# Attention of the later batches, one run a step or two runs every second step

## The chip, the cores and the metric

The kernel runs on one core of a Trainium2 chip. The metric is the device time of one execution in microseconds; the runs of a kernel are summarised by their median. A core has five engines that run beside each other, each through its own list of instructions in order: TensorE (PE in the profile, its weight loads PEld), VectorE (DVE), ScalarE (ACT), GpSimd (POOL) and SyncE (SP), which here issues the DMAs.

## The reference

Attention over 4 batches, 8 heads, 576 tokens and 64 dimensions, with a window of 32 keys: the first four heads see the last 32 keys ("plain"), the other four every fourth key of the last 128 ("dilated"). Two feed-forward blocks follow, over all 2304 tokens.

```python
scores = scale * np.matmul(q, k.transpose(0, 1, 3, 2))
scores = np.where(masks[None, :, :, :], scores, -1000000000.0)
attn = softmax(scores)                      # over the keys
x = np.matmul(attn, v)                      # then (tokens, 512)
x = ((x @ w_in) * np.cos(x @ w_in)) @ w_out # 512 -> 2048 -> 512
h = np.maximum(np.maximum(x @ w1, x @ w2), x @ w3)
return h @ w_out2                           # 512 -> 768 -> 512
```

## The kernel before

Attention is cut into 48 **runs** `(b, p, i)`: batch `b`, pair of heads `p` (0 and 1 plain, 2 and 3 dilated) and 192 queries `i`. A run has two query blocks of 96 and two heads, so four small problems of 96 queries by 128 keys. It goes through these operations, each a function of its own:

- `att_scores` (S): eight matmul instructions on TensorE at line 268 (four products in two passes each). The two heads lie in the two row halves of the array, and head `h` writes bank `6 + h` of PSUM. Then four reductions on VectorE (line 275) add the mask, take the row minimum of the negated scores and write the tile `e` in SBUF.
- `att_exp`: four exponentials on ScalarE (line 292, recorded at line 217). ScalarE loads a table when it goes from `Exp` to `Sin` or back, since the feed-forward block uses `Sin`.
- `att_norm`: an add, a reciprocal and one multiplication over `e` (lines 303 to 307).
- `att_T` (T): four transposes on TensorE (line 315) into one bank, and one copy to the tile `pt` (recorded at line 143).
- `att_out` (O): eight matmul instructions (line 326) into a bank, and then, for each piece of the destination, a copy and a subtraction into `ring` (lines 143 and 345). A dilated run has two or three pieces, a plain run mostly one. `att_done` calls it and then issues the load of the run five places on.

In the loop before, T of a run stands in bank 6 and O in bank 7; S uses both.

The first 12 runs are done ahead of the main loop. The main loop has 80 steps `s`, 16 for each of five token blocks (512 tokens, the last 256). A step has up to eight **chunks**: four "h" chunks of the first feed-forward product (three matmuls each, line 358) and four "a" chunks of the second (line 407) for the step three earlier. After the last h chunk `ff1_reduce` brings the argument into range on VectorE and ScalarE and issues the sine; `ff1_g` of the step before multiplies, and splits the product for the next matmul. In the second and third block `ff1_reduce` is done by VectorE in even steps and mostly by ScalarE in odd ones. In step `s` of the second to fourth block a piece of 256 columns of the last block's weights is also converted (lines 183, 443, 446).

The other 36 runs (12, 10, 12 and 2 of them during the first four blocks) are laid among the chunks. A run enters at the step that `LAST` spreads it to, which is nearly one run a step; its scores, transposes and outputs come at three places of a step, after the first, third and sixth chunk (T of the run three or two steps earlier, S of the new run, O of the earlier one). `GROUP` says how many runs share one `att_exp`: two in the first block, one in the others. The exponentials follow at the end of the step, the normalisation at the end of a later step.

The order in the code is a priority and not the order on the engines: the framework places instructions on an engine by that priority as they come ready, so that what waits is passed by what does not. It also adds the waits between engines, among them those on a PSUM bank that another engine reads.

Of the kernel before, what the change touches and what calls it, by code (L numbers as in the profile page):

```python
# [24 lines left out]
QB = 96  # L25
NQ = S // QB
KB = QB + WIN
# [3 lines left out]
NF1 = FF1 // 128  # L31
# [5 lines left out]
NBT = len(BLOCKS)  # L37
# [8 lines left out]
START = (3, 6, 7)  # L46
# [19 lines left out]
}  # L66


LAST = (13, 10, 12, 8)
GROUP = (2, 1, 1, 1, 1)  # L70

START_WEIGHTS = (0, 0, 2, 1, 0, 0, 0, 1, 0, 0, 1, 0, 1, 0, 1)
STEP_WEIGHTS = (
# [24 lines left out]
def body(  # L98
# [11 lines left out]
    nc = tc.nc  # L110
# [40 lines left out]
    bank = [ps.tile([128, 512], F32, name=f"bank{n}") for n in range(8)]  # L151
# [69 lines left out]
    given = {}  # L221
# [31 lines left out]
    places = {}  # L253
    HEADS = [(j, h) for j in range(2) for h in range(2)]

    def att_scores(u, n=None):
        b, p, i = u
        places[u] = (6, 7) if n is None else (START[2 * n % len(START)], START[(2 * n + 1) % len(START)])
        e = sp.tile([QB, 4, KB], F32, tag="e", name="e")

        m = smp.tile([QB, 4], F32, tag="m", name="m")
        places_of = {}
        for j, h in HEADS:
            q, k, _ = given[u][j]
            if n is None:
                rows = slice(64 * h, 64 * h + 64)
                sv = bank[6 + h][:QB, j * KB : j * KB + KB]
                nc.tensor.matmul(sv, q[rows], k[rows], start=True, stop=True)  # L268
            else:
                sv = bank[n % 3][:QB, (2 * j + h) * KB : (2 * j + h + 1) * KB]  # L270
                nc.tensor.matmul(sv, q[:, h * QB : (h + 1) * QB], k, start=True, stop=True)
            places_of[j, h] = sv
        for j, h in HEADS:
            kind = (PLAIN_KIND if p < 2 else DIL_KIND)[2 * i + j]
            nc.vector.tensor_tensor_reduce(  # L275
                out=e[:, 2 * j + h, :],
                in0=places_of[j, h],
                in1=mask[:, kind, :],
                scale=-1.0 / math.sqrt(D),
                scalar=3e38,  # L280
                op0=ALU.add,
                op1=ALU.min,
                accum_out=m[:, 2 * j + h : 2 * j + h + 1],
            )
        st[u] = e, m
# [547 lines left out]
    enter = {}  # L833
    for t, us in enumerate(plan[1:]):
        for i, u in enumerate(us):
            enter.setdefault(t * NF1 + i * LAST[t] // len(us), []).append(u)
    to_exp, to_norm, to_out = [], [], []
    NS = NBT * NF1
    hvs = {}
    for s in range(NS + LAG):  # L840
        phase[0] = 1 if s < NF1 else 2 if s < NS - NF1 else 3
        us = enter.get(s, [])
        assert s % NF1 or finished >= set(sum(plan[: s // NF1 + 1], []))
        if s == 0:
            weight_loads(WSLOTS, WSLOTS)

        vs = [to_out.pop(0) for _ in range(min(len(to_out), 1))]
        pieces = []
        for j in range(max(len(us), len(vs))):
            if j < len(vs):  # L850
                pieces.append((att_T, vs[j]))
            if j < len(us):
                pieces.append((att_scores, us[j]))
            if j < len(vs):
                pieces.append((att_done, vs[j]))
        chunks = []
        t, f = divmod(s, NF1)
        if s < NS:

            hv = (bank[3] if s == 2 else h_bank[(s + (s > 2)) % 2])[:, : BLOCKS[t]]  # L860
            hc = h_chunks(hv, halves[("in", f)], STARTS[t] % RING, BLOCKS[t])
            chunks += [("h", n, c) for n, c in enumerate((2, 3, 0, 1))]
        if s >= LAG:
            chunks += [("a", dm, 0) for dm in range(NC)]
        done = 0
        for j, (kind, x, c) in enumerate(chunks):
            if kind == "h":
                hc(x, c)
                if x == NC - 1:
                    hvs[s] = hv  # L870
                    ff1_reduce(s, hv)
            else:
                t0, f0 = divmod(s - LAG, NF1)
                acc_chunk(STARTS[t0], f0 == 0, f0 == NF1 - 1, halves[("out", f0)], g[s - LAG], x)
            while done < len(pieces) and done * len(chunks) < (j + 1) * len(pieces):
                do, u = pieces[done]
                do(u)
                done += 1
            if j == 1:
                if s >= 1 and s - 1 < NS:  # L880
                    ff1_g(s - 1)
            if s < NF1:
                weights(STEP_WEIGHTS[s].count(j), WSLOTS)
            if j == 1:
                raw_exponent(s - NF1)
            if j == 5:
                raw_bits(s - NF1)
        for u in us:
            to_exp.append(u)
        if to_norm:  # L890
            att_norm(to_norm, zt, tensor("norm"))
            to_out += to_norm
        to_norm = []
        if len(to_exp) >= GROUP[min(t, NBT - 1)] or (to_exp and s % NF1 >= LAST[min(t, len(LAST) - 1)]):
            zt = att_exp(to_exp)
            to_norm, to_exp = to_exp, []
        k = s - (NS - NF1)
        if k >= 0:
            ff2_early(k)
# [82 lines left out]
```

## Time and profile before

| | |
|---|---|
| time, median of 3 runs | 823.3 us (822.85 to 824.14) |
| profiled execution, span | 820.7 us |
| what lies around the span, median less span | 2.6 us |
| TensorE busy | 792.5 us, 97% |
| VectorE busy | 546.9 us, 67% |
| ScalarE busy | 463.7 us, 57% |
| GpSimd busy | 135.1 us, 16% |
| mean granted clock of TensorE | 0.983 of full speed |

The profile is of one execution, for which the span from its first to its last instruction is given; its own time is that span and what lies around it, which is taken from the runs. Busy times are unions of the engine's instructions. Matmuls are pipelined: a record lasts longer than the distance to the next one, so the price of a piece of TensorE's work is read from starts, not from durations.

### The profile page before, as it was taken

The page shows a single profiled execution, that of the slowest core. Times are in us where ns is not written, and L with a number is a line of the kernel's source. Part 1 is how long each engine was busy: PE and PEld are TensorE (multiplying, and loading weights), DVE is VectorE, ACT ScalarE, POOL GpSimd, SP SyncE. Part 2 cuts the span into 40 slices and gives each one's busy share as a digit, 9 for nine tenths or more (in the row PEclk, how much of TensorE's full clock was granted, in tenths as well). Part 3 has the DMA queues.
Part 4 walks back from the last instruction along what each step waited for, and adds up shares of the span by engine and source line. Part 5 has one row for each costly group of instructions (what it writes and reads, how often), then busy time and mean ns, then how long its engine had stood idle before and what let it go on. Part 6 is the DMA issues. An engine that isn't in the chain of part 4 may idle for free.

```text
span 820.7 us, 12988 instructions
## 1 busy us (share of the span) xinstructions
PE 792.5 (97%) x4484; PEld 679.5 (83%) x4484; DVE 546.9 (67%) x1442; ACT 463.7 (57%) x1063; POOL 135.1 (16%) x118
## 2 busy tenths in 40 slices
PE   8778999999999999999999999999999999999998
PEld 6556777777778777777788889998899999999997
DVE  5997698768886788876665477886872356515540
ACT  5787998868884488884553244364552233423321
POOL 2454345410000000000000002135510000000000
PEclk8987999999999999999999999999999999999999
DMA  9973111234344443332010025637683788448802
GB/s 350 419 283 142 39 48 52 73 113 148 117 129 130 128 163 112 115 121 84 27 45 10 0 94 183 238 144 271 239 311 106 225 248 263 150 135 254 253 26 77
DMA packets 52625, 124.43 MB, mean 152 GB/s; under 512 B 5840, under 2 KB 18768, under 8 KB 52560
## 3 DMA queue, kind: packets, MB, share of 16 engines
q1 hardware_dynamic: 52560, 123.61, 44.4%
q8 instruction: 35, 0.57, 0.3%
q14 instruction: 30, 0.25, 0.1%
HBM read 91.34 MB, written 32.24 MB: 151 GB/s over the span
## 4 chain that ended last, share of the span: by engine, by line
PE 77%; DVE 9%; DMA 8%; ACT 2%; issue 2%; POOL 1%; SPq 0%; DVEq 0%; ACTq 0%; POOLq 0%
PE bank L407 21%; PE bank L358 21%; PE bank L592 19%; PE bank L657 9%; DMA w<-in_w_in 4%; PE bank L268 4%; PE bank L326 2%; DMA raw<-wd 2%; PE bank L315 2%; DMA qkv<-in_qkv 2%; DVE ws L516 1%; DVE w L188 1%; POOL wa L491 1%; DVE e L307 1%; DVE wx L191 1%
## 5 line engine op out<-in xcount | busy, mean ns | idle before, releaser
L358 PE MATMUL bank<-ring,w 128*128 128x512 f32 (+1 forms) x960 | 236.1, 382 | 6.3 <-DVE r L396 5.1
L407 PE MATMUL bank<-gt,w 128*128 128x512 f32 (+1 forms) x960 | 223.7, 376 | 0.0
L592 PE MATMUL bank<-ring,wa 128*128 128x384 f32 x1134 | 201.3, 337 | 3.5 <-DVE mx L622 3.3
L592 PEld LDWEIGHTS bank<-ring,wa 128*128 128x128 f32 x1134 | 198.0, 189 | 5.1 <-DVE mx L622 4.1
L358 PEld LDWEIGHTS bank<-ring,w 128*128 128x128 f32 x960 | 165.2, 191 | 40.8 <-DVE r L396 6.6
L407 PEld LDWEIGHTS bank<-gt,w 128*128 128x128 f32 x960 | 165.8, 190 | 33.4 <-issue 0.6
L217 ACT ACTIVATE r<-r,hpi 128x512 f32<-128x512 f32 (+1 forms) x80 | 54.5, 681 | 70.0 <-DVE r L387 59.0
L217 ACT ACT_TABLE_LOAD x62 | 79.5, 1283 | 8.3 <-issue 3.4
L217 ACT ACTIVATE e<-e,m 96x128 f32<-96x128 f32 x192 | 74.8, 391 | 6.4 <-DVE m L275 6.0
L657 PE MATMUL bank<-g,w 128*128 128x384 f32 x432 | 76.3, 334 | 0.0
L657 PEld LDWEIGHTS bank<-g,w 128*128 128x128 f32 x432 | 75.0, 188 | 0.0
L396 DVE TENSOR_TENSOR r<-bank,r 128x512 f32<-128x512 f32 (+1 forms) x80 | 50.6, 632 | 27.2 <-ACT r L217 27.1
L139 POOL TENSOR_SCALAR gt<-r 128x512 fp32r<-128x512 f32 x24 | 16.3, 680 | 290.7 <-PE bank L407 132.5
L275 DVE CUSTOM_DVE_ANT_0 e<-bank,cs 96x128 f32<-96x128 f32 x192 | 44.9, 282 | 20.5 <-PE bank L268 9.2
L208 POOL TENSOR_TENSOR w<-wx,w 128x512 fp32r<-128x512 f32 x32 | 46.0, 1442 | 37.3 <-ACT w L143 34.0
L608 ACT COPY s<-bank 128x384 f32<-128x384 f32 x54 | 25.8, 478 | 39.0 <-PE bank L592 37.5
L398 DVE TENSOR_TENSOR gt<-r,gt 128x512 fp32r<-128x512 f32 (+1 forms) x65 | 40.3, 621 | 11.2 <-POOL gt L139 8.5
L626 DVE TENSOR_TENSOR s<-s,bank 128x384 f32<-128x384 f32 x36 | 19.8, 550 | 34.2 <-PE bank L592 34.2
L268 PEld LDWEIGHTS bank<-qkv 64*96 64x96 f32 x288 | 24.0, 168 | 20.2 <-issue 5.9
L626 DVE TENSOR_TENSOR mx<-s,bank 128x384 f32<-128x384 f32 x18 | 9.9, 550 | 43.2 <-PE bank L592 43.2
L382 DVE CUSTOM_DVE_ANT_0 r<-bank,r 128x512 f32<-128x512 f32 x40 | 27.4, 685 | 15.9 <-ACT r L381 15.7
L268 PE MATMUL bank<-qkv 64*96 64x128 f32 x288 | 35.4, 302 | 2.4 <-DVE m L275 2.4
(68 smaller groups left out, 908.7 us busy)
## 6 DMA issues: line engine op xcount, KB each, us to landing
wa<-opd SPq DMA_DIRECT2D x54, 512.0 KB, 4.5
opd<-wa SPq DMA_DIRECT2D x27, 512.0 KB, 3.0
qkv<-in_qkv SPq DMA_DIRECT2D x36, 336.0 KB, 2.9
wh<-in_w SPq DMA_DIRECT2D x36, 256.0 KB, 2.9
w<-in_w_in SPq DMA_DIRECT2D x16, 512.0 KB, 9.2
w<-in_w_out SPq DMA_DIRECT2D x16, 512.0 KB, 9.8
qkv<-in_qkv SPq DMA_DIRECT2D x12, 432.0 KB, 9.1
wd<-wh SPq DMA_DIRECT2D x36, 128.0 KB, 1.9
```

Of the source, the lines that this page charges most:

```text
L208: tensor("w_lo").tensor_tensor(out=w[:, 1, :], in0=x, in1=w[:, 0, :].bitcast(F32), op=ALU.subtract)
L217: last_table.append(nc.scalar.activation(*args, **kw).ins)
L268: nc.tensor.matmul(sv, q[rows], k[rows], start=True, stop=True)
L275: nc.vector.tensor_tensor_reduce(out=e[:, 2 * j + h, :], in0=places_of[j, h], in1=mask[:, kind, :], scale=-1.0 / math.sqrt(D), scalar=3e38 ...
L358: nc.tensor.matmul(hv, w[:, a, 128 * c : 128 * c + 128], ring[c][:, x, c0 : c0 + n_tok], start=n == 0 and j == 0, stop=n == NC - 1 and j == 2,
L382: nc.vector._custom_dve(dve_ops.TENSOR_ADD_SAT, out=r, in0=hv, in1=r, s0=ARG_HI, s1=ARG_LO)
L396: nc.vector.tensor_tensor(out=r, in0=hv, in1=r, op=ALU.mult)
L398: tensor("g_lo").tensor_tensor(out=gt[:, 1, :], in0=r, in1=gt[:, 0, :].bitcast(F32), op=ALU.subtract)
L407: nc.tensor.matmul(a_dm, w[:, a, 128 * dm : 128 * dm + 128], gt[:, x, :], start=first and n == 0, stop=last and n == 2,)
L592: nc.tensor.matmul(out, ops[q][a][:, x, 128 * c : 128 * c + 128], b_op(b, c)[:, y], start=first and c == 0 and n == 0, stop=c == 1 and n == 2,
L626: nc.vector.tensor_tensor(out=o, in0=y, in1=x, op=ALU.add)
L657: nc.tensor.matmul(a, wo[2 * f + r][:, x, 128 * dm : 128 * dm + 128], g2[f, r, n][:, y], start=f == 0 and r == 0 and k == 0, stop=f == NF2 ...
```

## The change

Runs enter in pairs at every second step. In such a step the transposes of both older runs stand together after the first chunk, the outputs of both after the fourth, and the scores of both new runs after the seventh. Run `k` of a pair now has bank `6 + k` for its transposes and its outputs; scores of head `h` stand in bank `6 + h` as before, the second run's 256 columns further. Exponentials of the pair follow at the end of the step, the normalisation at the end of the next, transposes and outputs in the one after that. `LAST` and `GROUP` go.

```diff
-LAST = (13, 10, 12, 8)
-GROUP = (2, 1, 1, 1, 1)
+PIECES = (0, 3, 6)
...
-    def att_scores(u, n=None):
+    def att_scores(u, n=None, k=0):
         b, p, i = u
-        places[u] = (6, 7) if n is None else (START[2 * n % len(START)], START[(2 * n + 1) % len(START)])
+        places[u] = (6 + k, 6 + k) if n is None else (START[2 * n % len(START)], START[(2 * n + 1) % len(START)])
...
-                sv = bank[6 + h][:QB, j * KB : j * KB + KB]
-                nc.tensor.matmul(sv, q[rows], k[rows], start=True, stop=True)
+                sv = bank[6 + h][:QB, (2 * k + j) * KB : (2 * k + j + 1) * KB]
+                nc.tensor.matmul(sv, q[rows], ks[rows], start=True, stop=True)
...
     for t, us in enumerate(plan[1:]):
         for i, u in enumerate(us):
-            enter.setdefault(t * NF1 + i * LAST[t] // len(us), []).append(u)
-    to_exp, to_norm, to_out = [], [], []
+            enter.setdefault(t * NF1 + i // 2 * 2, []).append(u)
+    to_norm, to_out = [], []
...
-        vs = [to_out.pop(0) for _ in range(min(len(to_out), 1))]
-        pieces = []
-        for j in range(max(len(us), len(vs))):
-            if j < len(vs):
-                pieces.append((att_T, vs[j]))
-            if j < len(us):
-                pieces.append((att_scores, us[j]))
-            if j < len(vs):
-                pieces.append((att_done, vs[j]))
+        vs, to_out = to_out, []
+        pieces = [
+            [(att_T, (v,)) for v in vs],
+            [(att_done, (v,)) for v in vs],
+            [(att_scores, (u, None, k)) for k, u in enumerate(us)],
+        ]
...
-            while done < len(pieces) and done * len(chunks) < (j + 1) * len(pieces):
-                do, u = pieces[done]
-                do(u)
-                done += 1
+            for at_chunk, piece in zip(PIECES, pieces):
+                if j == min(at_chunk, len(chunks) - 1):
+                    for do, args in piece:
+                        do(*args)
...
-        for u in us:
-            to_exp.append(u)
         if to_norm:
             att_norm(to_norm, zt, tensor("norm"))
-            to_out += to_norm
-        to_norm = []
-        if len(to_exp) >= GROUP[min(t, NBT - 1)] or (to_exp and s % NF1 >= LAST[min(t, len(LAST) - 1)]):
-            zt = att_exp(to_exp)
-            to_norm, to_exp = to_exp, []
+            to_out = to_norm
+        to_norm = us
+        if us:
+            zt = att_exp(us)
```

## Rows read from the trace of the kernel before

**Rows 1.** The page: the chain that ended last, by engine.
```profile
PE 77%; DVE 9%; DMA 8%; ACT 2%; issue 2%; POOL 1%; SPq 0%; DVEq 0%; ACTq 0%; POOLq 0%
```

**Rows 2.** Windows, first and third block: busy us by engine, granted clock, DMA, GB/s.
```profile
62.90:167.60 104.70, 100.33 (x545) 73.94 (x545) 80.56 (x214) 89.01 (x221) 45.51 (x33) 0.96 0.21 67
...
277.40:391.30 113.90, 113.46 (x626) 85.27 (x625) 90.03 (x292) 86.08 (x186) 5.77 (x8) 1.00 0.38 119
```

**Rows 3.** TensorE's timeline: start, length; first chunk of blocks two and five.
```profile
167.57 0.84 PE L358 MATMUL bank<-ring,w 128*128 128x512 f32 x3
...
482.30 1.60 PE L358 MATMUL bank<-ring,w 128*128 128x256 f32 x12
```

**Rows 4.** TensorE's timeline, a step without attention.
```profile
258.35 2.88 PE L407 MATMUL bank<-gt,w 128*128 128x512 f32 x12
...
263.79 1.07 PE L407 MATMUL bank<-gt,w 128*128 128x512 f32 x4
```

**Rows 5.** TensorE's timeline, the third block's first step: scores alone.
```profile
277.39 0.84 PE L358 MATMUL bank<-ring,w 128*128 128x512 f32 x3
278.16 0.68 PE L268 MATMUL bank<-qkv 64*96 64x128 f32 x8
...
283.66 0.84 PE L358 MATMUL bank<-ring,w 128*128 128x512 f32 x3
```

**Rows 6.** TensorE's timeline, a step with transposes and outputs alone.
```profile
403.00 0.84 PE L358 MATMUL bank<-ring,w 128*128 128x512 f32 x3
...
406.12 0.85 PE L407 MATMUL bank<-gt,w 128*128 128x512 f32 x3
...
409.58 0.63 PE L358 MATMUL bank<-ring,w 128*128 128x512 f32 x2
```

**Rows 7.** TensorE's timeline in narrow windows, inside one S and one O.
```profile
292.75 0.39 PE L268 MATMUL bank<-qkv 64*96 64x128 f32 x4
...
292.86 0.28 PE L268 MATMUL bank<-qkv 64*96 64x128 f32 x2
...
295.50 0.41 PE L326 MATMUL bank<-pt,qkv 128*64 128x96 f32 x5
...
295.58 0.34 PE L326 MATMUL bank<-pt,qkv 128*64 128x96 f32 x4
```

**Rows 8.** TensorE's timeline, one run's scores in two halves.
```profile
189.65 0.67 PE L268 MATMUL bank<-qkv 64*96 64x128 f32 x4
...
193.13 0.67 PE L268 MATMUL bank<-qkv 64*96 64x128 f32 x4
```

**Rows 9.** TensorE's waits between 62.9 and 482.3: in total, times, longest.
```profile
PE bank L268 <- DVE m L275: 2.4, 1, 2.4
```

**Rows 10.** The page's groups: count, busy us, mean ns, idle before.
```profile
L217 ACT ACT_TABLE_LOAD x62 | 79.5, 1283 | 8.3 <-issue 3.4
```

**Rows 11.** VectorE's timeline in an even step of the second block.
```profile
184.62 0.28 DVE L275 CUSTOM_DVE_ANT_0 e<-bank,cs 96x128 f32<-96x128 f32 x1
...
184.84 0.68 DVE L375 TENSOR_SCALAR kk<-bank 128x512 int32<-128x512 f32 x1
185.55 0.69 DVE L384 SCALAR_TENSOR_TENSOR r<-kk,bank 128x512 f32<-128x512 int32 x1
...
186.76 0.42 DVE L387 TENSOR_SCALAR r<-r 128x512 f32<-128x512 f32 x1
187.09 0.52 DVE L143 CAST ring<-bank 128x96 fp32r<-128x96 f32 x3
187.49 0.62 DVE L345 TENSOR_TENSOR ring<-bank,ring 128x96 fp32r<-128x96 f32 x3
```

**Rows 12.** Timeline of all engines, outputs of one run leaving bank 7.
```profile
97.27 0.52 ACT L143 CAST ring<-bank 128x48 fp32r<-128x48 f32 x2 [0.34 <-PE bank L326]
...
97.83 0.24 DVE L345 TENSOR_TENSOR ring<-bank,ring 128x48 fp32r<-128x48 f32 x1 [1.42 <-ACT ring L143]
```

**Rows 13.** The page's DMA issues: count, KB each, median us to landing.
```profile
qkv<-in_qkv SPq DMA_DIRECT2D x36, 336.0 KB, 2.9
```

More of the change, by code (lines that the diff above doesn't have):

```diff
@@ L263, in att_scores @@
         for j, h in HEADS:
-            q, k, _ = given[u][j]
+            q, ks, _ = given[u][j]
             if n is None:
                 rows = slice(64 * h, 64 * h + 64)
-                sv = bank[6 + h][:QB, j * KB : j * KB + KB]
-                nc.tensor.matmul(sv, q[rows], k[rows], start=True, stop=True)
+                sv = bank[6 + h][:QB, (2 * k + j) * KB : (2 * k + j + 1) * KB]
+                nc.tensor.matmul(sv, q[rows], ks[rows], start=True, stop=True)
             else:
                 sv = bank[n % 3][:QB, (2 * j + h) * KB : (2 * j + h + 1) * KB]
-                nc.tensor.matmul(sv, q[:, h * QB : (h + 1) * QB], k, start=True, stop=True)
+                nc.tensor.matmul(sv, q[:, h * QB : (h + 1) * QB], ks, start=True, stop=True)
             places_of[j, h] = sv
@@ L864, in body @@
             chunks += [("a", dm, 0) for dm in range(NC)]
-        done = 0
         for j, (kind, x, c) in enumerate(chunks):
```

## The prediction

> **What bounds the kernel now.** I read the chain that ended last first, to see which engine sets the time: TensorE has 77% of it, and no other engine comes near [rows 1]. Then the windows of the blocks that carry attention, to see whether that is work or waiting. In the first block TensorE is busy 100.3 of 104.7 us, in the third 113.5 of 113.9, at full clock there [rows 2]; VectorE and ScalarE are at 75 to 85% in both. So an instruction less on TensorE is worth its price, and one less elsewhere is worth nothing unless TensorE waited for it. Last I read TensorE's timeline step by step, for what attention adds to a step.
>
> A step without attention takes 5.44 us, so a chunk of three matmuls takes 0.68 [rows 4]. A step with scores alone takes 6.27: S costs 0.83 [rows 5]. In the step with T and O alone, the half that holds T takes 3.12 and the half that holds O 3.46, against 2.72 each: T costs 0.40, O 0.74 [rows 6]. A run that is not torn apart so costs 1.97.
>
> Most of S and O is not their instructions. Inside S a pair of instructions (one in each row half) starts every 0.11 us, inside O every 0.08 [rows 7]; four pairs are 0.44 and 0.32. The remaining 0.39 of S and 0.42 of O are paid for entering and leaving.
>
> The trace also shows scores in two halves with chunks between them, four instructions each, although the code issues all eight together [rows 8]. A half is as long as a whole (0.67 against 0.68 us) [rows 5, 8]: its four instructions use one row half, one after the other. So a torn S costs twice 0.83. Of the 36 runs 13 are torn, on my count over the timeline: six, four and three in the first three blocks. Halves tear because they wait for different banks: a bank is freed by the copy of T or by the copies of O, and a chunk that is ready is put ahead.
>
> **The sum before.** By terms: 36 x 1.97 = 70.9, and 13 x 0.83 = 10.8 for torn scores, together 81.7 us. By blocks: the second takes 109.8 us, 22.8 over 16 plain steps; the third and fourth together 204.9, 30.8 over 32 [rows 3, 5]. The first takes 104.7 [rows 2] against 78.2 (13 full and 3 half steps, less the first chunk), 26.5 over. Together 80.1, which includes 2.4 us of waiting for VectorE [rows 9]. The two agree within 2 us, so I price the change by terms.
>
> **The change, part by part.** 18 pairs take the place of 36 runs.
>
> *Transposes.* Four more in the same place. Four stand for 0.40 with their entry; the trace has no eight, so the second four cost between 0.32 (an O's four starts) and 0.40. I take 0.33, since a transpose uses the whole height like the chunks around it: 18 x 0.73 = 13.1 against 14.4. Where the second run's normalisation is late the two tear; that costs 0.07 a pair.
>
> *Outputs.* Both runs' banks differ (6 and 7), both `pt` tiles have buffers, and three chunks (2.04 us) lie between T and O, where before S wanted the copy after two. So I take them as joined: 0.74 + 0.32 = 1.06, 18 x 1.06 = 19.1 against 26.6. If they tear everywhere this is 26.6 again; that is the upper bound.
>
> *Scores of the first run.* They need both banks read out by the outputs of the pair before. O to S was nearly a whole step before; now three chunks lie between, 1.06 + 2.04 = 3.10 us from the start of O. VectorE first reduces the last h chunk, by itself in every even step of blocks two and three: from line 375 to the first copy 2.25 us, less 0.60 for another copy that comes between, so 1.65 [rows 11]. Three copies and three subtractions of a dilated run take 1.02 more [rows 11]. The first run's bank is then free 2.5 to 2.9 us after O starts, the second's 3.2 to 3.9: too late. With plain runs, about a third of that, both are free by 2.6. So after dilated outputs (nine pairs) I expect torn scores, 1.66; after plain ones (five) and at the head of a block (four) whole ones, 0.83. Together 22.4.
>
> *Scores of the second run.* They go to the same two banks, whose other columns the first run's reductions are reading. In the trace a subtraction on VectorE out of bank 7 starts at 97.83, 0.04 us after ScalarE's second copy out of that bank and not after the first, which holds its data, although VectorE had been idle for 1.42 us [rows 12]. One case, and the pieces also lie interleaved in `ring`; I read it as a bank being handed over whole. Then the second run's scores wait for at least three reductions, 0.21 us apart [rows 11], chunks go between, and the two runs' scores do not stand together. The banks come free 0.21 us apart, less than the 0.44 of a half, so the halves follow each other, but not side by side: 0.83 + 0.44 = 1.27, 18 x 1.27 = 22.9. Bounds 0.83 (whole) and 1.66 (torn).
>
> The Trainium skill, PSUM — Partial Sum Buffer, section "PSUM bank collisions raise a hardware error", says two engines may not touch one bank and quadrant of partitions at once, even in different columns, and to guard by bank. By that rule the joined scores that the change asks for cannot be had, and the sum is the one below; without it S would be 1.27 a pair and the sum 26.6 us less than before. The row above agrees; no run here tries the two at once.
>
> *ScalarE.* 62 table loads of 1.28 us [rows 10] are two for each of 30 groups of exponentials and two at the start. 18 groups leave 38: 24 x 1.28 = 30.8 us off ScalarE. TensorE's work hides it: ScalarE is idle 15 to 24% of these blocks [rows 2]. The loop of a pair (S, reductions, eight exponentials, normalisation, T, copies, O, `ring`, next S) must fit two steps, about 14 us; with shorter table time it fits, barely. If not, attention falls behind inside a block and has three or four spare steps there.
>
> *DMA.* Two loads of a run go out together every second step on SP's queue, with 2.9 us to landing [rows 13] and two to three steps before use: nothing. VectorE's and GpSimd's work stays.
>
> *Sum.* 13.1 + 19.1 + 22.4 + 22.9 = 77.5 against 81.7: 4.2 us less. The profiled execution has a span of 820.7, hence about 816.5; the median of the runs lies 2.6 above that span, so 823.3 becomes 819.1. I forecast 819.
>
> **The rivals.**
> *Scores torn everywhere.* Both runs at 1.66: 59.8 for S, total 92.0, 10.3 more than before: 834. For it: VectorE's list, with 1.65 us of reduction and the `ring` pieces ahead, is fuller in even steps than before. Against: plain outputs are short, and block heads wait for nothing. It decides from 2.75 us of S a pair; I reckon 2.52.
> *TensorE waits in place.* If nothing is put ahead of the scores, both runs stay whole (62.1 in all, 19.6 saved), but the second waits for four reductions (0.85) and the weights' conversion ahead of them (0.7), and the first up to 0.8 at nine pairs: 18 x 1.55 + 7 = 35, so 839. It decides from 1.1 us a pair. Against: chunks passed scores in the trace [rows 8], and TensorE waited 2.4 us for reductions, once [rows 9].
> *Whole but apart.* Every run's scores find both banks free: 1.66 a pair, total 62.1: 804. For it: before, 23 of 36 did.
> *All together, as the change says.* S 1.27 a pair, total 55.1: 797. Against: the shared banks.
> *ScalarE's relief reaches the end.* It can give back no more than TensorE's waiting, some 5 us [rows 2], on top of the forecast: 814. The Trainium skill, ScalarE: Activation LUTs, section "Table sets: the hidden batching unit", asks to batch by table set; the change does that, and ScalarE's 2% of the chain says how little it can be worth here.
>
> **How the numbers follow.** The measurement tells 0.2%, 1.65 us. Forecast 0.48, with 813 to 826 as its own range (second scores whole, or outputs and scores tearing more often); torn everywhere 0.17; waits in place 0.13; whole but apart 0.14; all together 0.03; relief 0.05. The range leaves out all together and waiting in place, 0.16: 803 to 835. Faster: three quarters of the forecast and the last three, 0.58; slower: both dear rivals and a little of the forecast, 0.31; same 0.11.
>
> **What would show it.** After: outputs of line 326 in groups of sixteen, transposes in eights, 38 table loads; line 268 never in sixteens, and halves of four after dilated outputs. The second block would take about 109 us instead of 109.8. If line 268 stands in sixteens, the bank step is wrong; if its idle time before is over 10 us, the waiting step; if outputs come in eights, the 7.5 us of them are not there. What would make the forecast wrong most: the tearing of scores, which I place by sums of durations within half a microsecond.

## The result and the profile after

The median went from 824.14 us (13 runs, 821.63 to 826.81) to 827.86 us (13 runs, 825.39 to 834.21), taken in turn on one chip: a ratio of 1.0058 [1.0041, 1.0075], slower by 0.6% (the medians alone give 1.0045). The profiled execution has a span of 826.0 us against 820.7. Its mean granted clock of TensorE is 0.988 of full speed against 0.983, so the clock as a whole is not what made it slower.

The page of the changed kernel: its busy times, the chain that ended last, and two of its groups:

```profile
PE 785.6 (95%) x4484; PEld 678.4 (82%) x4484; DVE 542.6 (66%) x1418; ACT 433.5 (52%) x1039; POOL 134.8 (16%) x118
...
PE 71%; DVE 12%; DMA 7%; ACT 5%; issue 3%; POOL 1%; SPq 0%; DVEq 0%; ACTq 0%; POOLq 0%
...
L216 ACT ACT_TABLE_LOAD x38 | 48.8, 1283 | 1.4 <-PEq L960 0.7
L267 PE MATMUL bank<-qkv 64*96 64x128 f32 x288 | 37.0, 290 | 8.2 <-DVE m L274 8.2
```

TensorE is busy for less time than before (785.6 us against 792.5; 3.4 of the 6.9 us lie in the four blocks below) and yet the end comes later; its share of the chain fell from 77% [rows 1] to 71%, and VectorE and ScalarE took what it lost. The table loads fell from 62 [rows 10] to 38, as the diff says. (Line numbers in the changed kernel are one less than in the kernel before; in the experiments they move again, and are named there.)

The windows by block tell busy time from waiting. The first starts at the loop's first scores, the others at the block's first chunk; columns as in [rows 2], PE first:

```profile
62.38:166.90 104.52, 95.18 (x544) 71.92 (x543) 80.39 (x213) 88.90 (x220) 46.15 (x34) 0.98 0.22 74
166.90:281.30 114.40, 110.38 (x584) 85.68 (x585) 84.41 (x267) 65.28 (x157) 7.41 (x10) 0.99 0.37 117
281.30:396.70 115.40, 115.10 (x625) 88.19 (x624) 88.39 (x278) 70.36 (x173) 4.95 (x8) 1.00 0.37 115
396.70:487.20 90.50, 90.50 (x425) 74.12 (x425) 53.77 (x107) 36.61 (x70) 4.97 (x8) 1.00 0.10 31
```

Length less PE's busy time is waiting: 9.3, 4.0, 0.3 and 0 us, 13.7 in all. Before, the four blocks had 414.6 us of work and 4.8 of waiting (4.4 of it in the first, [rows 2]); now they have 411.2 and 13.7. So TensorE's busy time fell by 3.4 us, near the 4.2 of the forecast, and 8.9 us of waiting came in. Block by block the kernel lost nothing in the first (104.5 against 104.7), 4.6 us in the second (114.4 against 109.8) and 1.5 in the third (115.4 against 113.9), this last without any waiting.

The waits of TensorE over these blocks (in total, times, longest):

```profile
PE bank L267 <- DVE m L274: 8.2, 3, 4.0
PE bank L314 <- DVE e L306: 4.5, 5, 1.0
PE bank L357 <- DVE r L395: 0.8, 1, 0.8
```

Two kinds of wait grew: scores for reductions, from 2.4 us [rows 9] to 8.2, and transposes for the normalisation, from 0.8 to 4.5. The largest of the first kind in the second block, on TensorE's timeline:

```profile
171.93 0.68 PE L267 MATMUL bank<-qkv 64*96 64x128 f32 x8
172.54 0.96 PE L406 MATMUL bank<-gt,w 128*128 128x512 f32 x3
173.34 0.40 PE L357 MATMUL bank<-ring,w 128*128 128x512 f32 x1
177.72 1.18 PE L267 MATMUL bank<-qkv 64*96 64x128 f32 x8 [3.98 <-DVE m L274]
178.82 4.06 PE L357 MATMUL bank<-ring,w 128*128 128x512 f32 x11
182.72 2.88 PE L406 MATMUL bank<-gt,w 128*128 128x512 f32 x12
```

The first run's scores stand at 171.93. The framework has put four matmuls between them and the second run's scores, which have to wait for the first run's reductions. This is not for want of other work: the h chunks of a step are twelve matmuls into one bank, the first of these twelve ran at 173.34, and the eleven behind the scores show no wait of their own. They stand behind the scores in TensorE's list, whose order was fixed when the kernel was built, and TensorE did not go past the scores that waited.

The wait also costs something after its end. The window of TensorE right behind it, columns as above:

```profile
177.72:181.60 3.88, 3.88 (x15) 3.02 (x16) 2.20 (x12) 3.87 (x17) 0.00 (x0) 0.56 0.51 169
```

The granted clock is 0.56 there, most of the stretch at the lower of its two levels (1.2 GHz instead of 2.4); in the kernel before the whole second block has 1.00. From the start of the scores to the next chunk it takes 1.10 us instead of 0.61, and the eleven matmuls take 3.90 instead of 2.5 (11 x 0.227): 1.9 us more on top of the 3.98.

VectorE's timeline tells where the first run's reductions were, and ScalarE's what held them:

```profile
172.80 0.68 DVE L374 TENSOR_SCALAR kk<-bank 128x512 int32<-128x512 f32 x1
174.81 0.29 DVE L442 TENSOR_SCALAR wh<-wh 128x256 int32<-128x256 int32 x1 [1.33 <-ACT wh L182]
175.02 0.68 DVE L383 SCALAR_TENSOR_TENSOR r<-kk,bank 128x512 f32<-128x512 int32 x1
175.62 0.42 DVE L445 SCALAR_TENSOR_TENSOR wh<-wh 128x256 int32<-128x256 int32 x1
175.95 0.42 DVE L386 TENSOR_SCALAR r<-r 128x512 f32<-128x512 f32 x1
176.29 0.29 DVE L442 TENSOR_SCALAR wh<-wh 128x256 int32<-128x256 int32 x1
176.61 0.43 DVE L445 SCALAR_TENSOR_TENSOR wh<-wh 128x256 int32<-128x256 int32 x1
176.95 0.28 DVE L274 CUSTOM_DVE_ANT_0 e<-bank,cs 96x128 f32<-96x128 f32 x1
```

```profile
174.34 0.43 ACT L182 ACTIVATE wh<-wh 128x256 f32<-128x256 f32 x1 [2.19 <-DMA wh<-in_w]
175.75 0.45 ACT L182 ACTIVATE wh<-wh 128x256 f32<-128x256 f32 x1 [0.97 <-DMA wh<-in_w]
```

The scores were there at 172.6, but the first reduction starts at 176.95. Ahead of it on VectorE stand two conversions of weight pieces of the last block; they wait for ScalarE's line 182, and that waits for a load of the weights. VectorE itself was idle for 1.33 us in front of work that could have run; the two conversions (1.4 us) and the reduction of an argument (1.8 us) make up the rest. So a load of something that the last block needs, 300 us later, helps to stop TensorE through the order of VectorE's list.

The third block loses without waiting. TensorE's timeline there, around one pair's scores:

```profile
326.97 0.82 PE L314 MATMUL bank<-cs,e 96*128 96x96 f32 x8
327.58 2.31 PE L357 MATMUL bank<-ring,w 128*128 128x512 f32 x9
329.82 0.88 PE L325 MATMUL bank<-pt,qkv 128*64 128x96 f32 x16
...
332.89 0.67 PE L267 MATMUL bank<-qkv 64*96 64x128 f32 x4
333.50 0.73 PE L406 MATMUL bank<-gt,w 128*128 128x512 f32 x2
334.16 0.67 PE L267 MATMUL bank<-qkv 64*96 64x128 f32 x4
334.76 0.51 PE L406 MATMUL bank<-gt,w 128*128 128x512 f32 x1
335.20 0.67 PE L267 MATMUL bank<-qkv 64*96 64x128 f32 x4
335.80 1.65 PE L357 MATMUL bank<-ring,w 128*128 128x512 f32 x6
337.38 0.67 PE L267 MATMUL bank<-qkv 64*96 64x128 f32 x4
```

Transposes stand in an eight and outputs in a sixteen, but the scores of the pair stand in four halves, each with its own entry and exit: 0.61 us from start to the next chunk each time, as long as a whole eight above (171.93 to 172.54). Counted over the timeline, 16 of 36 runs are torn now against 13 or 14 before, in a new distribution: 2, 5 and 9 in the first three blocks against 6, 4 and 3. Where the framework puts too little between the two runs' scores, TensorE waits (twice, in the first and second block); where it puts chunks between their halves, as in the third, the scores tear.

### The profile page after: what moved, and what is told of

The parts are those of the page before. It is cut to its first block, busy times and chain, and to the rows that moved or that the text cites. A ratio compares the mean times of both kernels' runs of the same rounds, so it can differ in the third digit from the quotient of the medians.

```text
span 826.0 us, 12917 instructions
## 1 busy us (share of the span) xinstructions
PE 785.6 (95%) x4484; PEld 678.4 (82%) x4484; DVE 542.6 (66%) x1418; ACT 433.5 (52%) x1039; POOL 134.8 (16%) x118
## 4 chain that ended last, share of the span: by engine, by line
PE 71%; DVE 12%; DMA 7%; ACT 5%; issue 3%; POOL 1%; SPq 0%; DVEq 0%; ACTq 0%; POOLq 0%
PE bank L591 20%; PE bank L357 18%; PE bank L406 18%; PE bank L656 9%; PE bank L267 3%; DMA wh<-in_w 2%; ACT e L216 2%; PE bank L325 2%; PE bank L314 2%; DMA raw<-wd 1%; DVE e L306 1%; DVE w L187 1%; DVE ws L515 1%; DVE wx L190 1%; POOL wa L490 1%
## 5 line engine op out<-in xcount | busy, mean ns | idle before, releaser
L357 PE MATMUL bank<-ring,w 128*128 128x512 f32 (+1 forms) x960 | 233.2, 382 | 5.7 <-DVE r L395 4.6
L406 PE MATMUL bank<-gt,w 128*128 128x512 f32 (+1 forms) x960 | 220.3, 375 | 0.0
L357 PEld LDWEIGHTS bank<-ring,w 128*128 128x128 f32 x960 | 167.3, 192 | 40.6 <-DVE r L395 5.9
L274 DVE CUSTOM_DVE_ANT_0 e<-bank,cs 96x128 f32<-96x128 f32 x192 | 45.1, 282 | 17.4 <-PE bank L267 8.7
L397 DVE TENSOR_TENSOR gt<-r,gt 128x512 fp32r<-128x512 f32 (+1 forms) x65 | 40.5, 623 | 17.1 <-POOL gt L138 8.9
L267 PEld LDWEIGHTS bank<-qkv 64*96 64x96 f32 x288 | 25.7, 159 | 26.6 <-DVE m L274 18.5
L381 DVE CUSTOM_DVE_ANT_0 r<-bank,r 128x512 f32<-128x512 f32 x40 | 27.4, 686 | 22.5 <-ACT r L380 22.3
```

Source lines behind the costliest of these rows:

```text
L267: nc.tensor.matmul(sv, q[rows], ks[rows], start=True, stop=True)
L274: nc.vector.tensor_tensor_reduce(out=e[:, 2 * j + h, :], in0=places_of[j, h], in1=mask[:, kind, :], scale=-1.0 / math.sqrt(D), scalar=3e38 ...
L357: nc.tensor.matmul(hv, w[:, a, 128 * c : 128 * c + 128], ring[c][:, x, c0 : c0 + n_tok], start=n == 0 and j == 0, stop=n == NC - 1 and j == 2,
L381: nc.vector._custom_dve(dve_ops.TENSOR_ADD_SAT, out=r, in0=hv, in1=r, s0=ARG_HI, s1=ARG_LO)
L397: tensor("g_lo").tensor_tensor(out=gt[:, 1, :], in0=r, in1=gt[:, 0, :].bitcast(F32), op=ALU.subtract)
L406: nc.tensor.matmul(a_dm, w[:, a, 128 * dm : 128 * dm + 128], gt[:, x, :], start=first and n == 0, stop=last and n == 2,)
```

## The experiments

The theory after the result: the second run's scores wait for the first run's reductions, because the two share both banks; what that costs is a wait where too little stands between and a tear where chunks do. The rivals: the exponentials of two runs together (later results for everything behind them), the transposes right behind the normalisation, and the weights' late loads by themselves. The loop's blocks are compared below from the reduction of the argument (line `kk`) in one block's last step to the next one's, the first block from its first. By this cut they take 111.4, 110.3, 113.0 and 91.2 us before, and 113.7, 110.6, 115.4 and 90.6 after. It puts a part of the second block's loss into the first, since after the change the `kk` at the seam stands on ScalarE behind a piece that waits 1.30 us for its load; by the windows above the loss is in the second. Ratios are to the kernel before, on the same chip. Block lengths are of the one profiled execution, which lies up to some 4 us from its kernel's median, so a difference of a microsecond in one block carries no weight.

**Both runs' products, then both runs' reductions** (from the changed kernel).

```diff
...
-            [(att_scores, (u, None, k)) for k, u in enumerate(us)],
+            [(att_scores, (u, None, k, what)) for what in ("product", "reduce") for k, u in enumerate(us)],
```

> The changed kernel, but the sixteen score instructions of both runs are issued first and the reductions of both after them, so the second run's scores no longer wait for the first run's reductions. Theory A (TensorE waits in place for reductions that stand behind late work in VectorE's list): the 4.0 us wait at 173.7 of the changed kernel and what it waits at 64 beyond the kernel before (1.6) go, span about 820. Theory B (torn scores): on top of that scores fall from 2.4 us a pair to 1.3 or, torn by bank, 2.5; with 11 of 18 pairs joined 43 us of scores become about 32, span about 810, faster than the kernel before by 1 to 1.5%. Theory C (late normalisation makes TensorE wait for the transposes): little changes, span above 822.

Measured: 828.36 us, 1.0070 [1.0046, 1.0095]. The scores stand in sixteens 11 times in 18, and the third block falls from 115.4 to 110.6: the tears were what it had lost. But the first block grows from 113.7 to 120.5. TensorE's waits in the loop (line 323 is the transposes here, line 366 the h chunks):

```profile
PE bank L323 <- DVE e L315: 17.6, 8, 7.3
PE bank L366 <- DVE r L404: 3.1, 1, 3.1
```

Not one wait of scores for reductions is left, and the transposes' wait for the normalisation is 17.6 us in place of 4.5. So the shared banks explain the tears and the scores' waits, but not the time: with them gone, the first block waits at the next place in the pair's loop. The mean granted clock over that block is 0.90 against 0.98 in the changed kernel, and three of its stretches at 1.2 GHz begin in or right behind the waits of 7.3, 1.8 and 3.0 us: these waits, too, cost more than they last.

**Weight pieces two steps later** (from the changed kernel).

```diff
-                raw_exponent(s - NF1)
+                raw_exponent(s - NF1 - 2)
-                raw_bits(s - NF1)
+                raw_bits(s - NF1 - 2)
```

> The changed kernel, but the conversion of the last block's weight pieces starts two steps later (from step 18 instead of 16), so nothing that depends on their DMA stands ahead of the first reductions of the second block. Theory A with the DMA as the late work: the 4.0 us wait in the second block's first pair goes, span about 822, all else equal. If the wait has another cause it stays, span 826.

Measured: 829.32 us, 1.0083 [1.0054, 1.0111]. The wait in the second block is 3.6 us at 172.6, and conversions still stand on VectorE from 168 to 175: the framework had put them forward again. The first conversion still comes at 158.7, in the first block (159.4 in the changed kernel). The run doesn't separate the load from the order; it shows that a place in the code doesn't decide what stands ahead of the reductions.

**The kernel before with exponentials of two runs together.**

```diff
-GROUP = (2, 1, 1, 1, 1)
+GROUP = (2, 2, 2, 2, 2)
```

> The kernel before with one part of the change: exponentials of two runs together in all blocks, scores, transposes and outputs one run at a time as before. Table loads fall by about two dozen (31 us off ScalarE). If ScalarE's table time only lies in the shade of TensorE, the time moves only with the scores that are torn: by the instruction order 8 instead of 13 or 14 runs, 5 x 0.83 = 4 us less, span about 816.5. If waiting for pairs is what costs (theory C), it is slower than before.

Measured: 820.55 us, 0.9976 [0.9952, 1.0000]; the scores are torn in 8 runs instead of 13. With 38 table loads, as in the changed kernel, it is no slower and may be a little faster; that rival falls, for exponentials without the rest of the change.

**The second run's scores one step after the first's** (from the changed kernel).

```diff
+    held = []
...
-            [(att_scores, (u, None, k)) for k, u in enumerate(us)],
+            [(att_scores, (u, None, k)) for k, u in enumerate(us[:1])] + [(att_scores, (u, None, 1)) for u in held[1:]],
         ]
+        us, held = held, us
```

> The changed kernel, but the second run's scores stand one step after the first's; transposes and outputs stay in pairs. Theory A: no reduction of the first run is waited for, the waits of 4 us go. Theory B: by the instruction order 6 runs torn instead of 16, 8 us less of scores, but only 11 outputs joined instead of 18, 3 us more. Together span about 813 to 817. Theory C: transposes still come in pairs right behind their normalisation, the waits of about 1 us each in the first block stay or grow.

Measured: 821.24 us, 0.9983 [0.9964, 1.0002]. Torn runs fall to 6, the third block to 110.7, and the scores' waits from 8.2 to 1.2 us, while those of the transposes for the normalisation grow to 6.8. The rest of the code stays, though outputs are now joined in only 11 pairs of 18, and the loss is gone: it hangs on the second run's scores standing right behind the first's.

**All weight conversions behind the last reductions on VectorE** (from the changed kernel; `last_red` is the newest reduction).

```diff
+    def behind_scores():
+        return tc.issue_after(last_red[0]) if last_red else nullcontext()
...
-                    do(order[k])
+                    with behind_scores():
+                        do(order[k])
...
-                raw_bits(s - NF1)
+                with behind_scores():
+                    raw_bits(s - NF1)
```

> The changed kernel, but on VectorE the conversions of weights that the code issues after a pair's scores are queued behind that pair's reductions (an order on one engine, no wait added or taken). Nothing else changes. Theory A: the two waits of 4.0 us before line 267 (at 64.2 and 173.7 of the changed kernel) shrink to about 1.5 and 0, since what stood ahead of the first run's reductions were conversions that waited for a DMA or ran slowly beside GpSimd; span about 819 to 820, faster than the changed kernel by 0.7%. Theory B (torn scores): the order on TensorE keeps its 16 torn runs, nothing gained, span 826.

Measured: 827.24 us, 1.0046 [1.0029, 1.0063]. The second block's waiting goes to nothing and its length from 110.6 to 108.0; the first grows from 113.7 to 117.1. The first pair of the loop, in the changed kernel (one line) and in this run (three; line 271 is the scores, line 319 the transposes):

```profile
68.15 0.88 PE L267 MATMUL bank<-qkv 64*96 64x128 f32 x8 [3.95 <-DVE m L274]
...
64.83 0.68 PE L271 MATMUL bank<-qkv 64*96 64x128 f32 x8
70.91 0.87 PE L319 MATMUL bank<-cs,e 96*128 96x96 f32 x4 [3.14 <-DVE e L311]
73.18 0.87 PE L319 MATMUL bank<-cs,e 96*128 96x96 f32 x4 [1.40 <-DVE e L311]
```

So here, too, the wait of the second run's scores hung on conversions ahead of the reductions: with these behind, it is gone. But the pair's transposes then wait 4.5 us for the normalisation. Two effects of opposite sign, so the first half of the edit is left out in a later run; why the whole block grows is not shown further.

**Transposes one chunk later** (from the changed kernel).

```diff
-PIECES = (0, 3, 6)
+PIECES = (1, 3, 6)
```

> The changed kernel with the transposes one chunk (0.68 us) later, after the second chunk instead of the first. Theory C: the four to five waits of 0.8 to 1.0 us before the second run's transposes in the first block become 0.1 to 0.3 each, 3.3 us less, span about 822.5; the copies and outputs behind them still have two chunks. If the transposes' waits are only the shadow of a slower VectorE, they move to the outputs (line 325 waits for the copies) and the span stays 826.

Measured: 830.82 us, 1.0084 [1.0055, 1.0114]. The transposes wait five times as before, 5.6 us in all instead of 4.5. As with the weights, a later place in the code did not take the wait away.

**Products, then reductions, with outputs one chunk earlier** (from the first experiment).

```diff
-PIECES = (0, 3, 6)
+PIECES = (0, 2, 6)
```

> The sixteen score instructions issued together as in e1_join, and the outputs one chunk earlier (after the third), so that the copies into ring have four chunks before the scores. By the instruction order 15 of 18 pairs' scores stand together instead of 11. Theory B: scores fall to 15 x 1.3 + 3 x 2.5 = 27 us from 43 in the changed kernel, span about 812. Theory A: TensorE waits in place for what is late on VectorE, as in e1_join (17.8 us idle in the loop), span 822 to 828, and the saved time of scores shows as idle time.

Measured: 817.16 us, 0.9937 [0.9919, 0.9955]. Scores stand in sixteens 15 times in 18. The third block takes 105.2 us, 10.2 less than in the changed kernel. A sixteen on TensorE's timeline there:

```profile
312.73 1.12 PE L269 MATMUL bank<-qkv 64*96 64x128 f32 x16
313.77 0.98 PE L415 MATMUL bank<-gt,w 128*128 128x512 f32 x3
```

It is 1.04 us from start to the next chunk, where four halves take 4 x 0.61 = 2.44. In the changed kernel the six pairs of this block stood in 18 halves and three wholes, 21 groups at about 0.83 or 17.4 us; as six sixteens, each 0.43 more than a whole, they cost 7.6. The difference, 9.8 us, is nearly all of the 10.2. The first block still has 16.7 us of waiting.

**The same with all conversions behind the reductions** (the previous kernel, with the edit of the fifth).

```diff
...
+                    with behind_scores():
+                        do(order[k])
...
+                with behind_scores():
+                    raw_bits(s - NF1)
```

> e7_join26 with VectorE's order of e5_order: scores together and conversions behind the reductions. If both theories hold together (tearing costs TensorE's time, and waits in place ate what joining saved), this one keeps both gains: span 806 to 812, faster than the kernel before by over 1%. If waits move on to the next thing that is late (transposes behind normalisation), it stays near 820.

Measured: 813.79 us, 0.9889 [0.9859, 0.9920]. The second block is 105.3 us without any waiting; the first is 114.1, with 15.4 us of it.

**One of GpSimd's pieces of the split moved to VectorE** (from the changed kernel).

```diff
-    "g_lo": ("P", "P", "V", "V"),
+    "g_lo": ("P", "V", "V", "V"),
```

> The changed kernel, but in the first block the second half of the product's split (line 397) is done by VectorE and not by GpSimd. In the changed kernel's trace VectorE's multiplication at line 306 takes 0.69 us alone and 1.76 us beside a GpSimd instruction. If that is why TensorE waits for the second run's transposes (theory C: four waits of 0.8 to 1.0 us in the first block), those waits go, though VectorE has 16 x 0.62 = 10 us more to do; the first block changes by little and its idle time is of another kind. If normalisation is late for VectorE's own load, those waits grow.

Measured: 831.72 us, 1.0121 [1.0097, 1.0144]; the first block takes 117.7. The waits of the transposes for the normalisation went from five to three, 1.53, 0.88 and 2.0 us. The last two follow a multiplication that stands beside GpSimd's other work (1.77 and 1.48 us); the first follows two that took 0.69 and 0.68. TensorE waits less in the first block than in the changed kernel (7.5 us against 9.3, from the loop's first scores on) and is busy 5.5 us longer, at a granted clock of 0.93 against 0.98. So the run prices neither the contention nor VectorE's larger load.

**Only the last block's weight pieces behind the reductions** (from the changed kernel).

```diff
...
-                raw_bits(s - NF1)
+                with behind_scores():
+                    raw_bits(s - NF1)
```

> The changed kernel with half of e5_order: only the weight pieces of blocks two to four are queued behind the reductions, the first block is untouched. Theory A: the second block's wait of 4.0 us goes and nothing else does, span about 822 to 823, time within 0.2% of the kernel before, so that the second block's wait is the larger part of what the change cost. If the wait moves on, the second block keeps its length and the time stays 0.5% above.

Measured: 821.89 us against 821.86, 1.0001 [0.9987, 1.0015]. This edit alone takes the whole loss back. TensorE's waits and the second run's scores at the place shown above (line 319 is the transposes, 271 the scores, 278 the reductions):

```profile
PE bank L319 <- DVE e L311: 3.9, 5, 1.0
PE bank L271 <- DVE m L278: 2.8, 2, 2.4
...
173.00 0.89 PE L271 MATMUL bank<-qkv 64*96 64x128 f32 x8 [0.41 <-DVE m L278]
```

The 3.98 us became 0.41, the granted clock of the second block is 1.00 again, and its length 107.2 us instead of 110.6; the first 112.0 instead of 113.7, the third 114.1 instead of 115.4. By the windows from chunk to chunk the second block takes 109.6 us, against 114.4 in the changed kernel and 109.8 before. The edit itself orders only VectorE's list, but the loads move with it. SyncE's issues in the changed kernel, a store of two converted pieces and the load of the next two:

```profile
169.22 1.93 SPq L448 DMA_DIRECT2D wd<-wh  x2
171.20 1.72 SPq L451 DMA_DIRECT2D wh<-in_w  x2
```

The pieces go round in two buffers: a load goes out once a conversion is done and its store has landed. So a conversion that is put early brings the next load early too, and the next conversion stands in VectorE's list waiting for it. In the tenth run no such load is issued between 161.6 and 177.2, where the changed kernel issues four. The run shows that the conversions ahead of the reductions are the cause; it does not part their own time from their wait for the load.

**The first block one run at a time, the others as in the seventh kernel with the edit before this.**

```diff
...
+            at_step = i * 13 // len(us) if t == 0 else i // 2 * 2
+            enter.setdefault(t * NF1 + at_step, []).append(u)
...
+        vs, to_out = (to_out[:1], to_out[1:]) if s < NF1 else (to_out, [])
...
+        if len(to_exp) >= 2 or (to_exp and s >= NF1):
```

> The first block as in the kernel before (one run at a time), the other blocks as in e8_join26_order: scores of both runs issued before their reductions, outputs after the third chunk, pieces behind the reductions. If the first block is where pairs cost (VectorE beside GpSimd, weights late), its length returns from 114 to about 111 us while blocks two and three stay at 105 to 106: span about 806 to 808, 1.5% faster than the kernel before. If the first block's length comes from elsewhere, 810.

Measured: 806.73 us against 821.86, 0.9813 [0.9789, 0.9837], the best of all. Windows of its first three blocks (cut at the line `kk`; columns as above):

```profile
53.33:165.13 111.80, 104.07 (x555) 76.09 (x554) 87.72 (x221) 96.16 (x234) 51.52 (x37) 0.95 0.28 94
165.13:269.58 104.45, 104.45 (x583) 83.63 (x582) 79.15 (x252) 61.00 (x150) 6.26 (x9) 1.00 0.34 107
269.58:375.40 105.82, 105.82 (x626) 84.61 (x625) 84.99 (x267) 68.41 (x167) 4.95 (x8) 1.00 0.33 105
```

Against the kernel before, the first block is the same (111.8 and 111.4), and the second and third are 5.8 and 7.2 us shorter, with no waiting at all. So pairs, with products before reductions, outputs a chunk earlier and the last block's pieces behind, are worth some 13 us in the two blocks where VectorE and ScalarE have room, and pairs gained nothing in the first, where ScalarE is busy 96 of 112 us and VectorE shares its time with the weights' conversion. What the order of the pieces alone gives the kernel before was not tried; its second block has no waiting for that order to take away.

## Why the prediction was wrong

**Transposes and outputs: right.** Outputs were joined 18 times in 18, at 1.01 us a pair (forecast 1.06). The transposes of ten pairs are in eights, at 0.70, and of the others in fours (forecast 0.73 a pair); the tears happen where the second run's normalisation is late.

**Table loads: right.** 38; the third run, which has the grouping alone and five torn runs fewer besides, is 0.24% faster (0 to 0.48%).

**Scores, as a count: right in size, not in place.** By pieces and prices, 20 whole at 0.83 and 32 halves at 0.81 are 42.5 us, against 22.4 + 22.9 = 45.3 in the forecast. With T and O the terms come to some 74 against 77.5. That would be 7.6 less than the 81.7 before; TensorE's busy time fell only by 3.4, though. Each block's length less its waits and less 0.227 us for each chunk matmul, against the sum of the prices: 23.1 and 21.1 us in the second, 28.0 and 27.4 in the third, 3.4 and 3.4 in the fourth, so the prices hold there once the 1.9 us at the lower clock behind the wait are taken off. In the first it is 26.5 and 22.3; a part of that also lies at the lower clock, behind the wait of 3.95, and the rest I have not assigned. In the third block, with nine of twelve torn, S is 18 x 0.81 + 3 x 0.83 = 17.1 for six pairs, 2.85 each: above the 2.75 at which the forecast turns, where it reckoned 2.52.

**The sum before, by blocks: right by luck.** The forecast set 78.2 us of chunks against the first block's 104.7. The window holds some 305 chunk matmuls (545 less 240 of attention, [rows 2]), which is 69 us at 0.227 each, so 35.6 were over and not 26.5. Of these 4.4 are waiting, and the granted clock of 0.96 means about 8 us at the lower level, an estimate of up to 4 us of slower work; the remaining 27 are near the 28.6 of the terms (12 x 1.97 and 6 x 0.83). So the prices stand, but the 26.5 came out by errors that cancel, and they hid the clock as a term of its own.

**"Chunks go between": this step failed.** In "Scores of the second run" I had them wait for the first run's reductions, rightly, and then priced that wait at nothing, because chunks had passed scores in the trace [rows 8]. Chunks go between only as far as the framework, which fixes the order when the kernel is built, has put them there. It put four matmuls there, and TensorE stood for 4 us before eleven more that show no wait of their own. Scores' waits went from 2.4 to 8.2 us, below the 10 that I had named as the mark; the step failed all the same, since the whole forecast gain was 4.2. The rival "TensorE waits in place" named the mechanism, with the weights' conversion ahead of the reductions at 0.7 us for each pair. What happened is rarer and dearer: two waits of 4.0, and a lower clock behind them, a cost that the forecast did not have at all. In the tenth run the one in the second block goes to 0.41 and the loss with it, so this is shown: the reductions stood behind conversions, which in the trace waited for a load. For the wait at 64.2 in the first block the fifth run shows the same: there conversions of weights (lines 187 and 190) stand ahead of the reductions on VectorE, two of line 187 taking 2.93 us together beside GpSimd against 0.42 each alone, and with the conversions behind the reductions the scores wait no longer, though the transposes then do.

**Transposes behind the normalisation: priced at 0.07 a pair.** I had asked whether they tear and not whether TensorE waits. The transposes of both runs need both normalisations, which are one behind the other on VectorE; the waits grew by 3.7 us. The timeline of all engines around one such wait:

```profile
95.58 2.38 DVE L306 TENSOR_TENSOR e<-e,z 96x512 f32<-96x512 f32 x2
95.69 1.72 POOL L397 TENSOR_TENSOR gt<-r,gt 128x512 fp32r<-128x512 f32 x1 [4.67 <-ACT gt L142]
...
96.50 0.49 PE L314 MATMUL bank<-cs,e 96*128 96x96 f32 x4
...
98.11 0.27 PE L314 MATMUL bank<-cs,e 96*128 96x96 f32 x1 [0.85 <-DVE e L306]
```

The two multiplications of the normalisation take 2.38 us here, while GpSimd works, against 1.29 at 72.72. The first run's transposes go at 96.50, the second's wait until 98.11. Without GpSimd the second multiplication would have been done about 1.1 us earlier, and the 0.85 would not be there; that is argued from durations, since the ninth run didn't isolate it. It can't be the whole: the 0.93 us before the transposes at 73.56 follows two multiplications that are not slowed.

**The rule on banks.** I had read it, and [rows 12], as a bar to joined scores. What tore them was only the reductions standing between the two runs' products: with all products first, scores stood in sixteens 15 times in 18. A sixteen costs 0.43 more than an eight (1.04 against 0.61 from start to the next chunk), where the forecast had 0.44; so the price of 1.27 for a joined pair was right, for an order that the change did not have. The Trainium skill, PSUM — Partial Sum Buffer, section "PSUM bank collisions raise a hardware error", asks to guard by bank; the order with all products first keeps that rule, and the scores stand joined under it.

**The rival "whole but apart"** was tried by itself in the fourth run: 0.2% below the kernel before and not the 804 that I gave it. Its terms were not reached: six runs were still torn, and seven pairs of outputs and thirteen of transposes were not joined, some 8 us by the prices; and TensorE waited 10 us in the four blocks against 4.8 before, since the waits of the transposes grew as the scores' waits went.

**What stays open.** Which part of the 3.98 us is the load and which the conversions' own time was not separated, nor why the framework puts conversions of the last block ahead of reductions that TensorE needs. The first block's waiting is not split between scores, normalisation and GpSimd; in the eleventh run it is back at its old size only because that block is handled as before. The cause of the lower clock was not tried by itself; the traces show only that here it came in or right behind the long waits.

## What to carry to other kernels

A wait that "other work will fill" costs nothing only if that work stands ahead of the wait in the engine's list, whose order is fixed before the run: compare what stands between with the longest thing that can stand ahead of the releaser, and look at the releaser's engine for an instruction that itself waits for a DMA. Look at the granted clock behind a long wait as well; here 3.98 us of waiting cost some 1.9 us more. Bunching work for an engine that pays for each change of shape pays only if what feeds the bunch is bunched too: first all products, then all reductions, with the banks freed early enough. And where stages have different slack, try the new order per stage: here it was worth 13 us in two blocks, and in the runs that had it in the first block too that block got longer.

## What the runs showed of the hardware

**A multiplication on VectorE beside GpSimd.** In the changed kernel line 306 (both operands in SBUF) takes 686 ns (median) in 33 cases alone. Of nine that overlap with an instruction of GpSimd, the five that start while it already runs take 1636 to 1784, and the four that start before it take 678 to 687. So for this line it counts which of the two starts first. Line 190 takes 681 alone and up to 1762 beside GpSimd, line 187 418 and up to 2498. Operations with an operand in PSUM do not change: line 274 282 in both cases, line 395 691, line 344 351 and 348. The Trainium skill, SBUF — State Buffer, section "Who interferes with whom", says that VectorE's second pair of ports is GpSimd's too, and that an instruction of VectorE with two inputs in SBUF contends with one of GpSimd that reads SBUF, and one in a mode with two ports with GpSimd, while one with at most a single SBUF input outside these modes does not. The durations agree. For a plan it means that VectorE's time in this first block can't be added up from durations taken elsewhere.

**TensorE's clock behind a wait.** Right behind the waits of 3.95 and 3.98 us the changed kernel has a stretch at the lower granted clock (1.2 GHz, a share of 0.50, from 68.94 to 72.36 us; 0.56 from 177.72 to 181.60), in which chunk matmuls start 0.43 us apart instead of 0.23. The second, sixth and ninth runs show the same about the second block's wait of 3.6 us. In the tenth, where that wait is 0.41 us, the whole second block has 1.00.
